# Cosine attention and a highway layer on one core: scores in 64x64 tiles, and a new order

## The chip, the core and the metric

The kernel runs on one core of one Trainium2 chip. The metric is the device time of one execution in microseconds. Engines are named as in the profile: PE (matrix products), PEld (its weight loads), DVE (VectorE), ACT (ScalarE), POOL (GpSimd), SP (SyncE, here only a queue of DMAs). A change of over 2% either way counts as faster or slower.

## The reference

```
q_n = q / (norm(q) + 1e-6);  k_n = k / (norm(k) + 1e-6)        # 8 batches, 12 heads, 448 tokens, 64 per head
attn = softmax(q_n @ k_n.T / tau)                              # tau 0.1
x = (attn @ v) as 3584 tokens x 768
out = T * relu(x @ w_h) + (1 - T) * x,   T = sigmoid(x @ w_t + b_t)
```

## The kernel before

Operands of the products are in fp16, sums in fp32. The work of a batch `b` is cut into 3 groups of 4 heads; a group holds two pairs `s` of heads, and the two heads `t` of a pair lie side by side in the partitions of the turned q and k (64 each). Tokens are split as `token = 7*l + j`, so 448 tokens are 7 blocks `j` of 64.

For each group: load q and k, square them (`sq`, ACT), sum (`rd`, DVE), inverse roots (`ln`/`ie` on ACT for batch 0, Newton steps `nt` on DVE later), scale to `qn` and `kn` (POOL mostly; `scale`), turn so that the 64 numbers of a head lie along the partitions (`turn`: on PE with a copy by DVE, or by a transposing DMA on SP for q from batch 3 and k from batch 5). Then for each pair: scores, transposed, as 128 keys x 448 queries (`qk`), exponentials by ACT (`exp`, tile `E`), products with v (`av` for three blocks of 128 queries, `avt` for the last 64), a division (`rc`, `ev` on DVE) into `x`. Column 64 of `vp` is one, so the same product gives the sum of the exponentials. Per head 448 keys are three blocks of 128 and one of 64. The 64 left over of both heads of a pair are put together: `kn` has an eighth block, half of it zero, so that one product with 128 rows (`qkt`, line 507, tile `Et`) gives the left-over scores of both heads.

PE runs in modes, named in the code: F is the whole array, T two tiles of 64 rows x 128 columns (the two heads of a pair at once), C two tiles of 128 rows x 64 columns.

Batch 0 is done in smaller pieces (`attend0`), one step for 128 queries, to get going early. `wm` and `wf` are products of zeros (tile `wz`) that fill PE's early gaps. Each batch's `x` (4 tiles of 128 tokens x 768, the last a half) goes through `ffn`: a transpose to `xT` (DMA on SP from batch 1), 24 products `ff` for T and H, then `za`, `hm`, `gt`, `gg` on DVE, `th` on ACT, `out` on POOL and a store on SP. The layer's work of a batch is spread over the attention of later ones.

Nothing is scheduled by rule: `ORDER` is a table of numbers that lists all operations in the order in which they are issued, `SLOTS` the buffer of each tile. Each engine runs its own part of this list in order. Two rules add waits without data: an SP load of q waits for the last ACT operation ahead of it in the list, and the first POOL operation of certain kinds behind a DVE operation of such kinds (`PORT`) waits for that one.

Of the kernel before, what the change touches and what calls it, by code (L numbers as in the profile page):

```python
# [126 lines left out]
    ),  # L127
}


# [733 lines left out]
```

## Time and profile before

| | |
|---|---|
| median of 3 runs | 255.94 us (255.06 to 262.05) |
| span of the profiled execution, first to last instruction | 252.9 us |
| PE, ACT, DVE, POOL busy, share of the span | 94%, 84%, 82%, 73% |
| PE matmuls | 2895 |
| PE's granted clock, mean | 0.990 |

The profile shows the span and not the profiled execution's whole time; the median of the runs is 3.0 us above that span, the lowest run 2.2 us. In the profile a matmul's duration includes the time until its result has drained, so durations of neighbours overlap and their sum says nothing: the cost of one is the distance from its start to the next one's start, called its pitch below.

### The profile page before, as it was taken

What the parts mean: (1) busy time and instruction counts of PE and PEld (TensorE: products, weight loads), DVE (VectorE), ACT (ScalarE), POOL (GpSimd) and SP (SyncE); (2) the same over time, 40 slices, a digit from 0 to 9 for tenths busy, and PEclk for the clock granted to TensorE, in tenths of its full rate; (3) what the DMA queues carried; (4) which work ended last, traced back from release to release, by engine and by line L of the source; (5) the groups of instructions that cost most, each with busy time, mean ns of one, the idle gap of its engine ahead of it and who ended that gap; (6) DMA issues with size and microseconds to landing.
All of it is one profiled execution on the core that took longest, in us unless ns stands there. A gap on an engine that the chain in (4) does not pass through costs nothing.

```text
span 252.9 us, 7457 instructions
## 1 busy us (share of the span) xinstructions
PE 237.5 (94%) x2895; PEld 147.1 (58%) x2895; DVE 208.0 (82%) x462; ACT 211.5 (84%) x421; POOL 184.0 (73%) x261
## 2 busy tenths in 40 slices
PE   5959999999999999989999999999999999999990
PEld 2425776557756665645765566656656655675650
DVE  4977989999999999989899869689767665556983
ACT  3589999999999999989999999999997669981120
POOL 8369599959798979796989775878476983522540
PEclk9997999999999999999999999999999999999998
DMA  6999999999589999999999998999779588745755
GB/s 219 286 270 237 288 259 202 200 271 179 72 104 146 314 264 248 151 223 163 266 157 170 156 114 138 249 207 193 128 129 231 93 135 192 162 127 123 187 147 156
DMA packets 75892, 47.78 MB, mean 189 GB/s; under 512 B 51536, under 2 KB 72656, under 8 KB 75856
## 3 DMA queue, kind: packets, MB, share of 16 engines
q1 hardware_dynamic: 55568, 33.86, 59.2%
q0 software_dynamic: 19856, 12.68, 37.1%
q10 hardware_dynamic: 432, 0.75, 0.8%
q8 instruction: 22, 0.36, 0.6%
q14 instruction: 14, 0.11, 0.1%
HBM read 38.34 MB, written 11.01 MB: 195 GB/s over the span
## 4 chain that ended last, share of the span: by engine, by line
PE 68%; DMA 11%; ACT 8%; DVE 7%; issue 2%; POOL 2%; SPq 0%; DVEq 0%; POOLq 0%; ACTq 0%
PE B L682 26%; PE B L496 10%; PE B L526 8%; DMA xT<-x 7%; PE B L679 5%; PE B L521 3%; DMA E<-in_k_dram 3%; PE B L447 3%; ACT E L502 3%; PE B L534 3%; PE B L507 2%; PE B L573 2%; ACT sq L380 2%; PE B L305 2%; DVE hm L720 1%
## 5 line engine op out<-in xcount | busy, mean ns | idle before, releaser
L502 ACT ACTIVATE E<-B 128x448 f16<-128x448 f32 x252 | 122.8, 612 | 9.6 <-PE B L496 8.6
L682 PEld LDWEIGHTS <-xT 128*128 128x128 f16 x576 | 52.1, 98 | 39.6 <-issue 6.9
L752 POOL TENSOR_TENSOR os<-x,hm 128x384 f32<-128x384 f16 x53 | 47.6, 912 | 29.8 <-DVE hm L747 21.3
L682 PE MATMUL B<-wh,xT 128*128 128x384 f16 x288 | 56.7, 326 | 0.6 <-DMA xT<-x 0.6
L682 PE MATMUL B<-wt,xT 128*128 128x384 f16 x288 | 55.0, 326 | 1.8 <-DMA xT<-x 1.4
L432 POOL TENSOR_TENSOR kn<-kr,y 128x192 f16<-128x192 f16 (+1 forms) x84 | 45.8, 562 | 10.6 <-DVE y L409 6.1
L391 DVE TENSOR_REDUCE n<-sq 128x14 f32<-128x896 f32 (+1 forms) x50 | 51.2, 1039 | 2.8 <-ACT sq L380 2.6
L432 POOL TENSOR_TENSOR qn<-qr,y 128x448 f16<-128x448 f32 x47 | 43.9, 946 | 9.1 <-ACT y L420 4.4
L526 PE MATMUL B<-vp,E 128*128 128x65 f16 x756 | 38.7, 193 | 0.0
L724 ACT ACTIVATE tt<-z 128x768 f16<-128x768 f32 (+1 forms) x32 | 26.3, 821 | 14.6 <-DVE z L711 14.5
L720 DVE SCALAR_TENSOR_TENSOR hm<-B,x 128x384 f16<-128x384 f32 x53 | 28.8, 549 | 8.4 <-PE B L682 3.9
L526 PEld LDWEIGHTS <-E 128*128 128x128 f16 x756 | 33.7, 98 | 3.2
L496 PE MATMUL B<-qT,kT 64*128 64x448 f16 x252 | 34.8, 354 | 0.4 <-DVE hm L720 0.4
L711 DVE TENSOR_TENSOR z<-B,bias 128x384 f32<-128x384 f32 x48 | 25.8, 551 | 9.3 <-PE B L682 6.3
L521 PE MATMUL B<-vp,Et 128*128 128x130 f16 x126 | 28.1, 223 | 0.0
L380 ACT ACTIVATE sq<-qr 128x896 f32<-128x896 f32 (+1 forms) x24 | 24.1, 1022 | 3.5 <-DMA qr<-in_q_dram 3.5
L509 ACT ACTIVATE Et<-B 128x448 f16<-128x448 f32 x42 | 26.1, 631 | 0.4 <-PE B L507 0.4
L542 DVE SCALAR_TENSOR_TENSOR x<-B,rd 128x448 f16<-128x448 f32 x42 | 25.6, 618 | 0.9
L337 POOL DMA_DIRECT2D vr<-in_v_dram x32 | 21.9, 690 | 2.5 <-DVE z L711 2.5
L586 ACT ACTIVATE E<-B 128x512 f16<-128x512 f32 (+1 forms) x42 | 20.6, 607 | 0.9 <-POOL qn L432 0.5
L380 ACT ACTIVATE sq<-kr 128x896 f32<-128x896 f16 x17 | 17.0, 1041 | 1.1 <-DMA kr<-in_k_dram 1.1
L305 PE MATMUL B<-wz 128*128 128x512 f16 x39 | 14.7, 433 | 2.6 <-DVE wz L281 2.6
(81 smaller groups left out, 313.7 us busy)
## 6 DMA issues: line engine op xcount, KB each, us to landing
out_dram<-os SPq DMA_DIRECT2D x47, 192.0 KB, 3.3
qr<-in_q_dram SPq DMA_DIRECT2D x6, 1344.0 KB, 8.3
kr<-in_k_dram POOLq DMA_DIRECT2D x7, 672.0 KB, 11.6
vr<-in_v_dram POOLq DMA_DIRECT2D x16, 192.0 KB, 6.9
qr<-in_q_dram SPq DMA_DIRECT2D x6, 448.0 KB, 10.0
vr<-in_v_dram POOLq DMA_DIRECT2D x16, 144.0 KB, 7.7
out_dram<-os SPq DMA_DIRECT2D x15, 96.0 KB, 3.8
wt<-in_moe_w_t_dram POOLq DMA_DIRECT2D x1, 1152.0 KB, 24.4
```

Source lines behind the costliest of these rows:

```text
L380: nc.scalar.activation(dst, src, AF.Square, scale=sc)
L391: nc.vector.reduce_sum(R("n2", b)[:, c : c + 7 * n], a, axis=AX.X)
L432: ENG[eng].tensor_mul(N[:, :, t, :] if nm == "q" else N[:, lo > 0 : (lo > 0) + 2 * (hi - lo) - 1 : 2, t, :], source(nm, b, g)[:, t, 64 * l ...
L496: nc.tensor.matmul(R("B", ("S", n, c, t))[:, 0:S], lhsT=R("kT", i)[ln, s, 128 * c : 128 * c + 128], rhs=queries(ln), start=True, stop=True)
L502: nc.scalar.activation(R("E", n)[:, at : at + 7, :].rearrange("l j x -> l (j x)"), R("B", ("S", n, c, t))[:, 0:S], AF.Exp)
L509: op("ACT", f"expt {n}", lambda: nc.scalar.activation(R("Et", n).rearrange("l j x -> l (j x)"), R("B", ("St", n))[:, 0:S], AF.Exp), r=[("B ...
L521: nc.tensor.matmul(U[:, 2 * c : 2 * c + 2, :], lhsT=Et[:, 2 * c : 2 * c + 2, :].rearrange("l j x -> l (j x)"), rhs=vp[:, 6:8, 0:65], start ...
L526: nc.tensor.matmul(U[:, 2 * c + t, :], lhsT=E[:, at : at + 2, :].rearrange("l j x -> l (j x)"), rhs=vp[:, 3 * t + m, 0:65], start=False, s ...
L682: nc.tensor.matmul(P[:, 0:MH], lhsT=xT[:, cc, :], rhs=w_[:, cc, MH * mh : MH * mh + MH], start=(cc == 0), stop=(cc == CC - 1))
L720: op("DVE", f"hm {g} {mh}", lambda at=at, sl=sl, mh=mh: nc.vector.scalar_tensor_tensor(out=R("hm", g)[:, sl], in0=R("B", at)[:, 0:MH], sca ...
L724: op("ACT", f"th{nb} {g}", lambda: nc.scalar.activation(R("tt", g)[:, 0:W], R("z", g)[:, 0:W], AF.Tanh, scale=0.5), r=[("z", g), ("t0",)], ...
L752: op(eng, f"out {g} {mh}", lambda sl=sl, mh=mh: ENG[eng].tensor_add(R("os", g)[:, sl], xpart(mh), R("hm", g)[:, sl]), r=[("gg", g), xk], w ...
```

## The change

The scores are now computed as four tiles of 64 keys x 64 rows at once (mode Q, `score`), two heads by two halves of the keys. The blocks of keys stay in the order of the tokens, `kn` has seven blocks and no zeros. The block that is left over is block 3 for pair 0 and block 6 for pair 1, so one step of four tiles (`tails`) gives the left-over scores of all four heads of a group: for each head `t` a bank of PSUM with pair 0 in the lower and pair 1 in the upper half, and `Et` is kept by group and head. `av` takes its left-over product per head (65 columns) instead of one for both (130). The zeros that this needs are in `vp`. `kn` is scaled in one instruction instead of two, k turned in 7 blocks instead of 8, and by one DMA instead of two.

```diff
-    WARM, NF, NLATE = 18, 39, 2
+    WARM, NF, NLATE = 18, 60, 2
-    SCALE = {("q", 0, 0): ("DVE", "POOL"), ("k", 0, 0): ("DVE", "POOL")}
+    SCALE = {(nm, 0, g): ("DVE", "POOL") for nm in "qk" for g in range(NG)}
...
-        Et=(3, [128, 7, 64], FP16), ...
+        Et=(4, [128, 7, 64], FP16), ...
...
-            for lo, hi in ((0, 7),) if nm == "q" else ((0, 4 - t), (4 - t, 7)):
...
+            def fn(t=t, eng=eng):
+                c = col(nm, g) + 7 * t
+                ENG[eng].tensor_mul(R(nm + "n", i)[:, :, t, :], source(nm, b, g)[:, t].rearrange("l (j d) -> l j d", d=D),
+                                    R("y", b)[:, c : c + NJ].unsqueeze(2).to_broadcast([128, NJ, D]))
...
+    def score(out, o, w, K, Q, s, c):
+        for t, h in ((0, 0), (1, 1), (0, 1), (1, 0)):
+            ln = slice(64 * t, 64 * t + 64)
+            S_, j = (s, c + h * (4 - s)) if c < NC else (h, 3 + 3 * h)
+            nc.tensor.matmul(out[t][64 * h : 64 * h + 64, o[t] : o[t] + w], lhsT=K[ln, j, S_, :], rhs=Q[ln, :, S_, :], start=True, stop=True)
...
-                for t in range(2):
-                    ln = slice(64 * t, 64 * t + 64)
-                    nc.tensor.matmul(R("B", ("S", n, c, t))[:, 0:S], lhsT=R("kT", i)[ln, s, 128 * c : 128 * c + 128],
-                                     rhs=queries(ln), start=True, stop=True)
+                score([R("B", ("S", n, c, t)) for t in range(2)], (0, 0), S, R("kT", i), R("qT", i), s, c)
...
-            nc.tensor.matmul(R("B", ("St", n))[:, 0:S], lhsT=R("kT", i)[:, s, 384:512], rhs=queries(slice(0, 128)), start=True, stop=True)
+            score([R("B", ("St", i, t)) for t in range(2)], (0, 0), S, R("kT", i), R("qT", i), 0, NC)
...
-            nc.tensor.matmul(U[:, 2 * c : 2 * c + 2, :], lhsT=Et[:, 2 * c : 2 * c + 2, :].rearrange("l j x -> l (j x)"),
-                             rhs=vp[:, 6:8, 0:65], start=True, stop=False)
             for t in range(2):
-                for m in range(NC):
...
+                for m in range(NC + 1):
+                    lt = E[:, 7 * (2 * m + t) + 2 * c :][:, 0:2] if m < NC else R("Et", (i, t))[:, 2 * c : 2 * c + 2]
...
-                    ld_kf(g, "SP" if g else "ACT")
+                    ld_kf(g, "ACT")
...
-            ld_qk("q", b)
+            for g in range(NG):
+                ld_qk("q", b, [g])
...
-                elif o.held:
-
-                    behind(made[0], act)
-                elif o.port and o.eng == "DVE":
-                    before = made[-1]
-                elif o.port and before is not None:
-
-                    behind(made[0], before)
-                    before = None
+                last[o.seq] = made[-1]
+                if o.seq in BEHIND:
+                    behind(made[0], last[BEHIND[o.seq]])
```

`BEHIND` is a table of 61 waits written out: 47 of a POOL operation for a DVE operation a few places ahead of it (the rule of before made 48), and 14 of an SP load of q for an ACT operation. v is loaded by pair instead of by head, with the same sizes. `ORDER` and `SLOTS` are new throughout:

```diff
-66 1 67 342 68 0 69 3 72 71 7 70 5 42 61 339 23 19 75 74 64 21 44 52 20 51 22 55 79 9 83 43 2 6 14 13 81 82 73 80 8 85
+0 84 92 4 2 9 86 13 345 16 88 5 85 17 12 3 91 14 87 6 18 1 89 7 22 8 10 93 20 21 15 90 11 97 99 19 23 349 24 98 25 26
```

Three places of the order follow. First PE, at a step of scores in the middle of the program; `kT` and `qT` are the turned operands, B the banks of PSUM. Before, two products for the two heads of a pair, then the left-over product of another pair:

```order
L496 LDWEIGHTS kT_90
L496 MATMUL B_124<-qT_89,kT_90 128x448
L496 LDWEIGHTS kT_90
L496 MATMUL B_128<-qT_89,kT_90 128x448
L507 LDWEIGHTS kT_91
L507 MATMUL B_123<-qT_87,kT_91 128x448
```

Now, one step (the four tiles of 64 keys alternate between the two heads' banks):

```order
L459 LDWEIGHTS kT_93
L459 MATMUL B_125<-qT_89,kT_93 64x448
L459 LDWEIGHTS kT_93
L459 MATMUL B_124<-qT_89,kT_93 64x448
L459 LDWEIGHTS kT_93
L459 MATMUL B_125<-qT_89,kT_93 64x448
L459 LDWEIGHTS kT_93
L459 MATMUL B_124<-qT_89,kT_93 64x448
```

There are 126 such steps for `qk` as before, and 21 instead of 42 steps for the left-over blocks, each now of this form.

Second POOL, at the scaling of batch 0 (`qn`, `kn` from the loads `qr` and `E`, which holds batch 0's k; `vr`, `vp` are v as loaded and as used). Before:

```order
L432 TENSOR_TENSOR qn_83<-qr_61,y_78 128x7x64
L432 TENSOR_TENSOR kn_66<-E_94,y_78 128x4x64
L432 TENSOR_TENSOR kn_66<-E_94,y_78 128x3x64
L432 TENSOR_TENSOR qn_84<-qr_61,y_78 128x7x64
L432 TENSOR_TENSOR kn_67<-E_95,y_78 128x4x64
L432 TENSOR_TENSOR qn_84<-qr_61,y_78 128x7x64
L432 TENSOR_TENSOR kn_67<-E_95,y_78 128x3x64
L478 COPY vp_71<-vr_69 64x6x64
L432 TENSOR_TENSOR kn_67<-E_95,y_78 128x3x64
L432 TENSOR_TENSOR kn_67<-E_95,y_78 128x4x64
```

Now:

```order
L433 TENSOR_TENSOR qn_83<-qr_61,y_78 128x7x64
L433 TENSOR_TENSOR kn_66<-E_94,y_78 128x7x64
L325 DMA kr_64<-in_k_dram 128x6x448
L433 TENSOR_TENSOR qn_84<-qr_61,y_78 128x7x64
L433 TENSOR_TENSOR kn_67<-E_95,y_78 128x7x64
L433 TENSOR_TENSOR kn_68<-E_96,y_78 128x7x64
L433 TENSOR_TENSOR qn_85<-qr_61,y_78 128x7x64
L474 COPY vp_71<-vr_69 64x2x3x64
```

The other half of groups 1 and 2 (`qn_84`, `kn_67`, `qn_85`, `kn_68`) went to DVE, and the copy of v stands behind all of the scaling.

Third SP, around the transposes of batch 2's `x`. Before:

```order
L322 DMA qr_61<-in_q_dram 128x6x448
L759 DMA out_dram<-os_120 64x384 x2
L762 DMA out_dram<-os_117 64x768 x2
L662 DMA_TRANSPOSE xT_106<-x_103 128x6x128
L662 DMA_TRANSPOSE xT_109<-x_103 128x6x128
L662 DMA_TRANSPOSE xT_105<-x_103 128x6x128
L762 DMA out_dram<-os_119 64x768 x2
L662 DMA_TRANSPOSE xT_107<-x_103 128x3x128
```

Now:

```order
L327 DMA qr_61<-in_q_dram 128x2x448
L442 DMA_TRANSPOSE qT_86<-qn_85 128x7x128
L746 DMA out_dram<-os_120 64x768 x2
L327 DMA qr_61<-in_q_dram 128x2x448 x2
L646 DMA_TRANSPOSE xT_107<-x_104 128x6x128
L646 DMA_TRANSPOSE xT_110<-x_104 128x6x128
L646 DMA_TRANSPOSE xT_109<-x_104 128x6x128
L746 DMA out_dram<-os_118 64x768 x2
```

The load of q is in three parts, with a transpose and stores between them. At the start of the program, PE now has 44 products of zeros ahead of its first transpose, before 34, and the other 11 of the 21 added ones stand among the work of batch 0; the tile of zeros is the first that DVE writes, before it came behind one `vp`. The three loads of batch 0's k are issued by ACT behind its table load; before, one was issued by ACT ahead of it and two by SP.

More of the change, by code (lines that the diff above doesn't have):

```diff
@@ new lines @@
+    "qT": "01232013210310230123013",
+    "kT": "01232013201320123012301",
+    "E": "012012102101021002210210202102120102120210212021021021102",
+    "Et": "012301230101230123012301230123012301230123",
+    "rd": "010101010101011010101001010101010101010101010101010101",
+    "x": "012012012",
+    "xT": "01234012340214302130421304321430",
+    "z": "01011010100010101011010110010101",
+    "tt": "01010101001100101011010001001011",
+    "hm": "01202021012110121022102120010210",
+    "os": "01231200132032302033020201320321",
@@ L131 @@
+BEHIND = dict(
+    map(int, n.split(":"))
+    for n in """
[5 rows of a table added]
+""".split()
+)
 PORT = ("nt", "gt", "gg", "vc", "qn", "kn", "vt", "out", "cx", "ou")
@@ L440, in turn @@
         at = ("T" + nm, i)
-        nj = NJ if nm == "q" else 8
-        def fn():
-            T = R16(at)[:, 0 : 128 * nj].rearrange("p (s j l) -> p j s l", s=2, j=nj)
-            for j in range(nj):
-                nc.tensor.transpose(T[:, j], R(nm + "n", i)[:, j].rearrange("l t d -> l (t d)"), ident[:, :])
-        if nm == "q" and b in QDMA:
-            op("SP", f"xd7 {b} {g}", lambda: nc.sync.dma_start(
-                R("qT", i).rearrange("p s x -> p (s x)").rearrange("p (j x) -> p j x", j=NJ),
-                R("qn", i).rearrange("l j t d -> l (j t d)"), transpose=True), r=[("qn", i, 0), ("qn", i, 1)], w=[tn(nm, i)])
-            return
@@ L453, in turn @@
-        if nm == "k" and b in KDMA:
-            for s in range(2):
-                op("SP", f"xdk {b} {g} {s}", lambda s=s: nc.sync.dma_start(
-                    R("kT", i)[:, s, :].rearrange("p (j x) -> p j x", j=8),
-                    R("kn", i)[64 * s : 64 * s + 64].rearrange("l j t d -> l (j t d)"), transpose=True),
-                   r=[("kn", i, 0), ("kn", i, 1), ("zkn",)], w=[tn(nm, i)])
-            return
-        op("PE", f"t{nm} {b} {g}", fn, r=[(nm + "n", i, 0), (nm + "n", i, 1), ("id",)] + ([("zkn",)] if nm == "k" else [])
+        if b in (QDMA if nm == "q" else KDMA):
+            op("SP", f"xd7{nm} {b} {g}", lambda: nc.sync.dma_start(
+                R(nm + "T", i).rearrange("p j s l -> p j (s l)"),
+                R(nm + "n", i).rearrange("l j t d -> l (j t d)"), transpose=True), r=[(nm + "n", i, 0), (nm + "n", i, 1)], w=[tn(nm, i)])
+            return
@@ L461, in turn @@
+        def fn():
+            for j in range(NJ):
+                nc.tensor.transpose(R16(at)[:, 128 * j : 128 * j + 128], R(nm + "n", i)[:, j].rearrange("l t d -> l (t d)"), ident[:, :])
+        op("PE", f"t{nm} {b} {g}", fn, r=[(nm + "n", i, 0), (nm + "n", i, 1), ("id",)]
            + ([("wm",)] if i == 0 and nm == "k" else []), w=[("B", at)], mode="F")
         op("DVE", f"cp{nm} {b} {g}", lambda: nc.vector.tensor_copy(
-            turned(nm, i), R16(at)[:, 0 : 128 * nj].rearrange("p (s x) -> p s x", s=2)), r=[("B", at)], w=[tn(nm, i)])
+            turned(nm, i).rearrange("p j s l -> p (j s l)"), R16(at)[:, 0:896]), r=[("B", at)], w=[tn(nm, i)])
@@ L550, in attend0, with at @@
     def attend0(g, i):
-        q_, k_ = turned_of(g)
-        w = 128 if i < 3 else 64
+        K_, Q_ = lambda: turned("k", g), lambda: turned("q", g)
+        nj = 2 if i < 3 else 1
+        w = 64 * nj
         e = ("q0", g, i)
-        def unit(s):
-            o = 896 * s if i < 3 else 0
-            h = 0 if i < 3 else 192 * s
-            return [[o + 512 * t + h + w * c for c in range(NC)] for t in range(2)], o + 384 + (0 if i < 3 else 64 * s)
+        def at(s, t, m):
+            if i < 3:
+                return (0, 768)[s] + (384, 512)[s] * t + w * m if m < NC else 768 + 512 * t + 384
+            return 448 * t + (192 * s + w * m if m < NC else 384)
@@ L561, in flat, with queries, fq @@
         def flat():
             return R("E", e).rearrange("l j x -> l (j x)")
+        def queries():
+            return Q_()[:, 2 * i : 2 * i + nj]
         for ss in ((0,), (1,)) if i < 3 else ((0, 1),):
-            A, B_ = (("S0", g, i, ss[0], t) for t in range(2))
-            o = unit(ss[0])[0][0][0]
-            def fq(ss=ss, A=A, B_=B_, o=o):
+            A = [("S0", g, i, ss[0], t) for t in range(2)]
+            base = [at(ss[0], t, 0) for t in range(2)]
+            M = 384 if ss == (0,) else 512 if ss == (1,) else 448
+            def fq(ss=ss, A=A, base=base):
@@ L581, in attend0 @@
-            n = f"{g} {i} {ss[0]}"
-            op("PE", f"qk0{len(ss)} {n}", fq, r=[tn("q", g), tn("k", g)],
-               w=[("B", A), ("B", B_)], mode="T")
-            op("PE", f"qt0{len(ss)} {n}", ft, r=[tn("q", g), tn("k", g)], w=[("B", A, "t")], mode="F")
-            for t, X, m in ((0, A, 512), (1, B_, 384)):
-                op("ACT", f"ex{m} {n}", lambda X=X, m=m, t=t, o=o: nc.scalar.activation(
-                    flat()[:, o + 512 * t : o + 512 * t + m], R("B", X)[:, 0:m], AF.Exp),
-                   r=[("B", X)] + ([("B", X, "t")] if t == 0 else []), w=[("E", e, s) for s in ss])
+                        score([R("B", a) for a in A], [at(s, t, c) - base[t] for t in range(2)], w, K_(), queries(), s, c)
@@ new lines, in ft @@
+            def ft(A=A, base=base):
+                score([R("B", a) for a in A], [at(0, t, NC) - base[t] for t in range(2)], w, K_(), queries(), 0, NC)
+            n = f"{g} {i} {ss[0]}"
+            op("PE", f"qk0{len(ss)} {n}", fq, r=[tn("q", g), tn("k", g)], w=[("B", a) for a in A], mode="Q")
+            if ss != (0,):
+                op("PE", f"qt0{len(ss)} {n}", ft, r=[tn("q", g), tn("k", g)], w=[("B", a, "t") for a in A], mode="Q")
+            for t in range(2):
+                op("ACT", f"ex{M} {n} {t}", lambda X=A[t], M=M, o=base[t]: nc.scalar.activation(
+                    flat()[:, o : o + M], R("B", X)[:, 0:M], AF.Exp),
+                   r=[("B", A[t])] + ([("B", A[t], "t")] if ss != (0,) else []), w=[("E", e, s) for s in ss])
@@ L595, in full @@
                 def full(s=s):
-                    vp, U, (at, tl) = R("vp", 0)[:, 2 * g + s], U_(), unit(s)
-                    nc.tensor.matmul(U[:, :, s], lhsT=flat()[:, tl : tl + 128], rhs=vp[:, 6:8, 0:65], start=True, stop=False)
+                    vp, U = R("vp", 0)[:, 2 * g + s], U_()
                     for t in range(2):
-                        for m in range(NC):
-                            nc.tensor.matmul(U[:, t, s], lhsT=flat()[:, at[t][m] : at[t][m] + 128],
-                                             rhs=vp[:, 3 * t + m, 0:65], start=False, stop=(t == 1 and m == NC - 1))
-                op("PE", f"av0 {g} {i} {s}", full, r=[("E", e, s), ("vp", 0, 2 * g + s), ("vp", 0, 6)], w=[("B", u)], mode="F")
+                        for m in range(NC + 1):
+                            a = at(s, t, m)
+                            nc.tensor.matmul(U[:, t, s], lhsT=flat()[:, a : a + w], rhs=vp[:, 3 * t + m if m < NC else 6 + t, 0:65],
+                                             start=(m == 0), stop=(m == NC))
+                op("PE", f"av0 {g} {i} {s}", full, r=[("E", e, 0), ("E", e, 1), ("vp", 0, 2 * g + s), ("vp", 0, 6, s)], w=[("B", u)], mode="F")
             op("DVE", f"rc {g} {i} 0", lambda: nc.vector.reciprocal(
@@ L632, in attend0 @@
                r=[("B", u), ("rd", e)], w=[("x", 0, i)])
-    def turned_of(g):
-        return lambda: turned("q", g), lambda: turned("k", g)
     def ffn(b, i):
@@ L801 @@
             for p in range(NP):
+                if p % 2 == 0:
+                    tails(b, p // 2)
                 scores(b, p)
@@ L812 @@
         with tc.manual_schedule():
-            before = act = None
+            last = {}
             for o in pl.ordered(ORDER, SLOTS):
```

122 lines of the change are left out of this document (46 added, 76 removed), and 149 rows, old and new, of tables (BEHIND, ORDER).

## The prediction

> **What bounds the kernel now.** I read the head of the page first.
>
> ```profile
> span 252.9 us, 7457 instructions
> PE 237.5 (94%) x2895; PEld 147.1 (58%) x2895; DVE 208.0 (82%) x462; ACT 211.5 (84%) x421; POOL 184.0 (73%) x261
> ```
>
> Then busy time in stretches of 10 us (columns: PE, PEld, DVE, ACT, POOL busy with the number of instructions, granted clock, DMA share, GB/s).
>
> ```profile
> 20.00:30.00 10.00, 10.00 (x140) 6.38 (x138) 9.24 (x23) 9.12 (x19) 6.90 (x11) 0.86 1.14 265
> 60.00:70.00 10.00, 10.00 (x175) 7.17 (x173) 9.46 (x20) 10.00 (x23) 8.57 (x14) 1.00 0.72 94
> 100.00:110.00 10.00, 8.55 (x107) 5.11 (x104) 9.72 (x25) 9.49 (x19) 8.54 (x13) 1.00 1.09 161
> 190.00:200.00 10.00, 9.56 (x118) 5.97 (x117) 6.98 (x13) 8.26 (x19) 7.32 (x10) 1.00 1.13 198
> 230.00:240.00 10.00, 10.00 (x64) 6.04 (x62) 8.34 (x18) 1.78 (x3) 5.14 (x6) 1.00 0.79 183
> ```
>
> Behind the start PE is hardly ever idle, and at 230 it works alone on the layer that is left: it sets the end. But ACT is as full through the middle, so PE cannot simply go ahead. Pitches decide, so I took a piece of PE's timeline (start, length, then the group).
>
> ```profile
> 186.06 0.22 PE L521 MATMUL B<-vp,Et 128*128 128x130 f16 x1
> 186.12 0.35 PE L526 MATMUL B<-vp,E 128*128 128x65 f16 x6
> 186.31 0.35 PE L507 MATMUL B<-qT,kT 128*128 128x448 f16 x1
> 186.59 0.28 PE L534 MATMUL B<-vp,E 128*64 128x65 f16 x6
> 186.71 0.20 PE L534 MATMUL B<-vp,Et 128*64 128x65 f16 x2
> 186.84 0.74 PE L496 MATMUL B<-qT,kT 64*128 64x448 f16 x6
> 187.51 3.10 PE L682 MATMUL B<-wt,xT 128*128 128x384 f16 x18
> 190.45 0.35 PE L507 MATMUL B<-qT,kT 128*128 128x448 f16 x1
> 190.64 0.22 PE L521 MATMUL B<-vp,Et 128*128 128x130 f16 x1
> ```
>
> From starts alone: a left-over product takes 0.19 us (190.45 to 190.64) and 0.28 where the next one is in another mode (186.31 to 186.59), so a change of mode costs 0.09. Three pairs of score products take 0.67, less 0.09 is 0.19 a pair: two tiles cost what one product does. The 18 layer products have 0.163 each. An `av` block is 0.25: 0.06 for the 130 columns and 0.19 for six of 65, 0.032 each. The eight products of `avt` take 0.25 less 0.09, 0.02 each.
>
> **The change on PE.** Left-over steps: 42 x 0.19 = 8.0 us go and 21 x 0.19 = 4.0 come, if four tiles of 64x64 run at once as two of 64x128 do: -4.0. The 126 `qk` steps stay at 0.19 on the same condition. An `av` block becomes eight products of 65 columns, 0.256 for 0.25: 126 + 18 blocks x 0.006 = +0.9. Batch 0's scores are 84 short steps for 96, at much the same few hundredths each: 0, give or take 1. Changes of mode, counted along both written orders, are 184 before and 182 now: -0.2.
>
> ```profile
> 36.08 0.45 PE B L447 x8
> ```
>
> In the chain of work eight transposes take 0.45 us, so the fifteen eighth blocks of k that go are worth 15 x 0.056 = -0.8. Together PE's work falls by 4.1 us, beside the products of zeros.
>
> The four tiles at once are what no row shows, and bounds are far apart: nothing extra, or a second round of 0.19 for each of 147 steps, 28 us. Two tiles beside each other in rows (`qk`) and two in columns (`avt`, two outputs at once) both run at full rate, so I take nothing extra.
>
> [...]
>
> **How much of it reaches the end.** ACT's pitches:
>
> ```profile
> 101.69 1.98 ACT L502 ACTIVATE E<-B 128x448 f16<-128x448 f32 x4
> 103.38 1.11 ACT L380 ACTIVATE sq<-qr 128x896 f32<-128x896 f32 x1
> 104.22 1.14 ACT L502 ACTIVATE E<-B 128x448 f16<-128x448 f32 x2
> ...
> 108.03 1.02 ACT L724 ACTIVATE tt<-z 128x768 f16<-128x768 f32 x1
> 108.77 0.72 ACT L509 ACTIVATE Et<-B 128x448 f16<-128x448 f32 x1
> ```
>
> An exponential is 0.42 us, a square 0.84, a tanh 0.74. Their numbers are the same before and after (252 + 42 exponentials of 448 columns, batch 0's again with the same columns in all). So there is a second bound: ACT's work up to some exponential, and from there PE's work from the first product that needs it. Priced with these pitches along both orders, the largest such sum is 230.2 us before (in the middle, at pair 17) and 228.8 now. By this bound only 1.4 of the 4.1 us come through; the rest sits where PE waits for ACT. I take 1.4, with 4.1 as the other end, since ACT's full rows say that this chain is tight.
>
> **Stalls in the middle.** PE loses time at three places:
>
> ```profile
> 106.64 0.35 PE L507 MATMUL B<-qT,kT 128*128 128x448 f16 x1
> 108.43 0.34 PE L682 MATMUL B<-wt,xT 128*128 128x384 f16 x1 [1.45 <-DMA xT<-x]
> 140.54 0.35 PE L526 MATMUL B<-vp,E 128*128 128x65 f16 x6
> 141.45 0.66 PE L682 MATMUL B<-wh,xT 128*128 128x384 f16 x3 [0.56 <-DMA xT<-x]
> 197.18 0.35 PE L496 MATMUL B<-qT,kT 64*128 64x448 f16 x1 [0.44 <-DVE hm L720]
> ```
>
> And the transposes of `x` about the first place (issue time on SP, then the time to landing):
>
> ```profile
> L662 SPq DMA_TRANSPOSE xT<-x x4: 1211/1238/1256, 98.1 to 102.1; - x4
> DMA to landing us min/median/max: 2.8/5.5/8.7
> ```
>
> Two of them end on a transposed `x` that came late: 1.6 us and 0.7 us of starts; the third is 0.4. At the first, transposes issued from 98.1 on took up to 8.7 us to land. The new order leaves them more room: PE work between the issue of a transpose of `x` and its first use, priced as above, is at least 3.4 us and 7.5 in the median, before 0.9 and 6.0; for turned q and k the least is 5.6, before 4.3. That q comes in thirds lets SP put transposes between them; what else is gained there by fewer DMAs (9 of k for 18, 1.24 us of SP each) meets 12 more issues of loads. I take 2.5 us of 2.7 gone; the other end is a loss of 2, since a new order can put a late landing somewhere else, and 8.7 us is longer than most of that room.
>
> **The start.**
>
> ```profile
> 9.59 1.05 DVE L432 TENSOR_TENSOR qn<-qr,y 128x448 f16<-128x448 f32 x1
> 17.30 0.57 ACT L586 ACTIVATE E<-B 128x512 f16<-128x512 f32 x1
> 17.73 0.50 POOL L478 COPY vp<-vr 64x384 f16<-64x384 f16 x1 [1.95 <-DMA vr<-in_v_dram]
> 18.19 1.53 POOL L432 TENSOR_TENSOR kn<-E,y 128x192 f16<-128x192 f32 x3
> 19.32 1.03 PE L447 MATMUL B<-ident,kn 128*128 128x128 f16 x8 [2.54 <-POOL kn L432]
> L285 ACT ACT_TABLE_LOAD x2 | 2.6, 1283 | 1.3 <-PEq L845 1.3
> ```
>
> Before, POOL stood 1.95 us at the copy of v with half of a k behind it, and PE waited 2.54 us for that (then came the low clock of 20 to 30). Now the copy is behind the scaling and DVE has half of it, so this wait goes. Next late is DVE: four more products of 1.05 us, 4.2, among its sums and copies, which is more than the 2.54 that PE waited; so I do not count the second group's k as earlier. Ten more products of zeros ahead of the first transpose, at
>
> ```profile
> 9.29 0.81 PE L305 MATMUL B<-wz 128*128 128x512 f16 x3
> 9.94 0.38 PE L301 MATMUL B<-wz 128*128 128x512 f16 x1
> ```
>
> 0.22 us each, hold it back by 2.2 us at most (PE starts sooner, its tile of zeros being the first that DVE writes); ACT's first exponential, at 17.30 behind squares that it had to do anyway, hides that, and if this cover is gone it costs what is left of the 2.2. The three loads of k behind ACT's table load may come later by its length, 1.28 us. The other eleven zeros, 2.4 us, lie in gaps in which PE waits for ACT. I take -0.5 us, between -2.5 and +1.5.
>
> **POOL** is off the path:
>
> ```profile
> L432 POOL TENSOR_TENSOR kn<-kr,y 128x256 f16<-128x256 f16 x42 | 25.4, 612 | 3.8 <-DVE hm L747 2.3 <-DVE y L409 1.2 <-DVE tt L726 0.3
> L432 POOL TENSOR_TENSOR kn<-kr,y 128x192 f16<-128x192 f16 x42 | 21.3, 512 | 6.7 <-DVE y L409 4.8 <-DVE tt L726 1.2 <-DVE hm L747 0.5
> ```
>
> 64 columns more cost 100 ns, so one of 448 is 0.91 us where two were 1.12: 42 times, 9 us less work. It has 27% idle time, so I count nothing. The written waits of POOL for DVE (47 for 48) change little.
>
> **Sum.** -1.4 (chain) - 2.5 (stalls) - 0.5 (start) = -4.4 us: the span goes from 252.9 to 248.5, and with the 3.0 us between span and median, 255.9 to **251.5 us**.
>
> **Rivals.**
> - *PE alone sets the pace*: all 4.1 us come through and the start gives its 2.5 us: -4.1 - 2.5 - 2.5 = -9.1, some of it overlapping: about 247.5 us. For it: at 190 to 200 ACT is idle and takes up slack. Against: ACT's full rows before that.
> - *The order does not hold on the chip*: new late landings cost 2 us instead of saving 2.5, start +1: 255.9 - 1.4 + 2 + 1 = 257.5, down to 254 where only one happens. For it: landings of 8.7 us.
> [...]
> - *Slower: the four tiles run in two rounds*, because two column tiles of one row half cannot stream at once. Price 0.19 us for each of 147 steps: 251.5 + 28 = 279 us. It decides from 65 ns more per step on: (4.4 + 5.1) / 147. For it: no row has all four. Against: either half alone runs at full rate.
>
> **How the numbers follow.** Forecast 0.52 (249 to 254), PE alone 0.17 (246 to 250), order 0.16 (254 to 258), loads 0.09 (253.5 to 257), two rounds 0.06. From 247 to 257.5 leaves out 0.06 above with two rounds, and about 0.12 at both edges. Two per cent, about what a measurement of this kernel can tell from no change, is 5.1 us: faster means under 250.8, which PE alone and two fifths of the forecast give, 0.17 + 0.21 = 0.38; slower means over 261, two rounds and a little of a bad order, 0.08; the same 0.54.
>
> **What would show it.** Right: a step of four tiles with a pitch of 0.19 us and its starts within some 20 ns, no PE wait of over 1 us for `xT`, no wait of PE for POOL at the start, ACT as full as before from 30 to 190, POOL busy some 10 us less. Wrong: steps of 0.21 or 0.38 us; a first exponential of batch 0 later than 17.3; ACT with idle time in the middle, which would mean that PE or a DMA sets the pace and my 1.4 is too small or the stalls moved.

## The result

The changed kernel takes **251.6 us** (251.11 to 252.33 in five runs); before, 255.94. The ratio is 0.989, with a 95% interval of 0.985 to 0.993, and two more comparisons with other runs gave 0.987 [0.983, 0.991] and 0.990 [0.984, 0.995]. So it is 1.1% faster, within the 2% that count as no change here, and its median is 0.1 us from the forecast. Medians count every execution and ratios leave out the slow ones, among them one of 573.8 us of the changed kernel, whose profile is not read here; by the ratio the gain is 2.8 us (1.7 to 3.8). The span went from 252.9 to 249.6 us, 3.3 us less. The other microsecond between the two medians is not the kernel's work: in every execution whose span is on record, of either kernel, the time is 1.7 to 1.9 us above that span. So the profiled execution of before took about 254.7 us (an estimate from its span), 1.2 us less than the median of 255.94.

The head of the page after:

```profile
span 249.6 us, 8704 instructions
PE 238.2 (95%) x3507; PEld 149.2 (60%) x3507; DVE 207.2 (83%) x459; ACT 211.0 (85%) x421; POOL 173.1 (69%) x210
```

POOL is busy 10.9 us less, where 9 were priced. PE has 612 products more and is as full as before. The same five stretches of 10 us (PE, PEld, DVE, ACT, POOL, granted clock, DMA share, GB/s):

```profile
20.00:30.00 10.00, 8.99 (x206) 5.59 (x204) 9.21 (x25) 10.00 (x19) 5.36 (x8) 1.00 1.14 273
60.00:70.00 10.00, 10.00 (x185) 6.89 (x184) 9.86 (x19) 10.00 (x23) 8.84 (x11) 1.00 0.96 159
100.00:110.00 10.00, 9.94 (x145) 6.53 (x145) 9.79 (x23) 10.00 (x22) 8.00 (x11) 1.00 1.24 136
190.00:200.00 10.00, 10.00 (x173) 6.37 (x173) 5.94 (x13) 9.27 (x21) 8.52 (x11) 1.00 1.22 193
230.00:240.00 10.00, 10.00 (x63) 6.02 (x62) 9.03 (x21) 3.37 (x4) 4.33 (x5) 1.00 0.59 147
```

The low clock of 20 to 30 (0.86) is gone, and PE and ACT are now both full at 100. Where the time came out can be followed from the starts of the exponentials of full blocks (252 in all, read from the records):

```
exponential no.      1     36     72    108    144    180    216    252   end of PE
before            42.7   67.7   94.8  122.0  148.0  175.3  199.3  225.7   246.5
after             41.0   69.7   95.5  121.9  148.3  173.0  197.4  222.2   243.4
```

By these starts alone nothing is gained up to the 144th, at 148 us. But the new order also puts ACT's other work in other places, so what ACT has still ahead of it has to be counted in. At the start of the 36th exponential that is 152.9 us before and 151.2 now, at the 108th 99.8 and 99.0, at the 144th 74.7 and 72.5. With it, the changed kernel is 0.3 us behind at the 36th, 0.9 ahead at the 108th, 1.9 ahead at the 144th and 3.1 at the end of PE. Between the 36th and the 144th ACT stood idle for 2.1 us before and does not now. The largest of these waits came right behind the late transpose of `x` that held PE at 108.43 us:

```profile
110.65 0.54 ACT L502 ACTIVATE E<-B 128x448 f16<-128x448 f32 x1 [1.16 <-PE B L496]
```

Three steps of four tiles in PE's timeline after (start, length, group):

```profile
190.87 0.76 PE L459 MATMUL B<-qT,kT 64*64 64x448 f16 x12
191.56 0.28 PE L525 MATMUL B<-vp,E 128*64 128x65 f16 x6
```

Twelve products in 0.69 us, where six took 0.67 before (186.84 to 187.51). Four tiles of 64x64 run at once. Over the steps that another step follows, the pitch has two values: 213 ns for the first step behind a change of mode (53 steps), 189 for the ones behind it (27, and two longer ones). Before it was 200 and 189. The first and the last start of a step lie 10 ns apart in the median. A product's record is longer than its pitch (a left-over product of before 353 ns in the mean, at 190 from start to start); what the rest of the record covers, no run shows.

One kind of gap is new. At three places PE stops in the middle of an operation, and no releaser is named but its own issue:

```profile
28.84 0.39 PE L589 MATMUL B<-vp,E 128*128 128x65 f16 x7
30.05 0.20 PE L589 MATMUL B<-vp,E 128*128 128x65 f16 x1 [0.82 <-issue]
...
35.16 0.46 PE L459 MATMUL B<-x 64*64 64x128 f16 x24
36.24 0.32 PE L459 MATMUL B<-x 64*64 64x64 f16 x16 [0.63 <-issue]
...
57.61 0.41 PE L612 MATMUL B<-vp,E 128*64 128x65 f16 x14
58.87 0.22 PE L612 MATMUL B<-vp,E 128*64 128x65 f16 x2 [0.85 <-issue]
```

One late transpose of `x` holds PE now, at another place, and for less:

```profile
206.28 0.99 PE L666 MATMUL B<-wt,xT 128*128 128x384 f16 x5 [0.56 <-DMA xT<-x]
```

At the start ACT's first exponential came 1.8 us earlier (15.51 for 17.30), and DVE's scaling of 448 columns took 0.62 us where it took 1.05:

```profile
10.10 0.62 DVE L433 TENSOR_TENSOR qn<-qr,y 128x448 f16<-128x448 f32 x1
...
15.51 1.85 ACT L575 ACTIVATE E<-B 128x512 f16<-128x512 f32 x4 [1.35 <-PE B L459]
```

### The profile page after: what moved, and what is told of

It is laid out like the page before. It is cut to its first block, busy times and chain, and to the rows that moved or that the text cites. A ratio compares the mean times of both kernels' runs of the same rounds, so it can differ in the third digit from the quotient of the medians.

```text
span 249.6 us, 8704 instructions
## 1 busy us (share of the span) xinstructions
PE 238.2 (95%) x3507; PEld 149.2 (60%) x3507; DVE 207.2 (83%) x459; ACT 211.0 (85%) x421; POOL 173.1 (69%) x210
## 4 chain that ended last, share of the span: by engine, by line
PE 64%; DMA 9%; ACT 9%; DVE 8%; POOL 4%; issue 3%; SPq 1%; DVEq 0%; ACTq 0%
PE B L666 31%; PE B L459 12%; PE B L517 11%; DMA qr<-in_q_dram 7%; ACT E L489 4%; PE B L663 3%; PE B L449 3%; PE B L525 3%; POOL qn L433 2%; ACT E L575 2%; DMA xT<-x 2%; DVE z L695 2%; ACT sq L383 2%; POOL kn L433 1%; PE B L589 1%
## 5 line engine op out<-in xcount | busy, mean ns | idle before, releaser
L489 ACT ACTIVATE E<-B 128x448 f16<-128x448 f32 x252 | 124.9, 666 | 5.6 <-PE B L459 5.4
L433 POOL TENSOR_TENSOR qn<-qr,y 128x448 f16<-128x448 f32 x45 | 41.5, 935 | 17.3 <-DVE y L412 7.0
L459 PE MATMUL B<-qT,kT 64*64 64x448 f16 (+2 forms) x812 | 47.1, 320 | 0.1
L433 POOL TENSOR_TENSOR kn<-kr,y 128x448 f16<-128x448 f16 x42 | 39.1, 938 | 5.6 <-DVE tu L408 2.0
L517 PEld LDWEIGHTS <-E 128*128 128x128 f16 x756 | 35.0, 97 | 7.6 <-issue 3.4
L517 PE MATMUL B<-vp,Et 128*128 128x65 f16 x252 | 35.0, 191 | 0.0
L459 PEld LDWEIGHTS <-kT 64*64 64x64 f16 x812 | 19.3, 105 | 19.0 <-issue 12.2
L383 ACT ACTIVATE sq<-qr 128x896 f32<-128x896 f32 (+1 forms) x24 | 25.8, 1073 | 5.6 <-DMA qr<-in_q_dram 5.4
L517 PEld LDWEIGHTS <-Et 128*128 128x128 f16 x252 | 24.8, 99 | 0.0
L575 ACT ACTIVATE E<-B 128x512 f16<-128x512 f32 (+2 forms) x42 | 20.3, 580 | 2.1 <-PE B L459 1.9
```

The source lines that it names most:

```text
L383: nc.scalar.activation(dst, src, AF.Square, scale=sc)
L433: ENG[eng].tensor_mul(R(nm + "n", i)[:, :, t, :], source(nm, b, g)[:, t].rearrange("l (j d) -> l j d", d=D), R("y", b)[:, c : c + NJ].unsq ...
L459: nc.tensor.matmul(out[t][64 * h : 64 * h + 64, o[t] : o[t] + w], lhsT=K[ln, j, S_, :], rhs=Q[ln, :, S_, :], start=True, stop=True)
L489: nc.scalar.activation(R("E", n)[:, at : at + 7, :].rearrange("l j x -> l (j x)"), R("B", ("S", n, c, t))[:, 0:S], AF.Exp)
L517: nc.tensor.matmul(U[:, 2 * c + t, :], lhsT=lt.rearrange("l j x -> l (j x)"), rhs=vp[:, 3 * t + m if m < NC else 6 + t, 0:65], start=(m == ...
```

## The experiments

Each starts from the changed kernel. Ratios are to the kernel before on the same chip; without an edit the ratio is 0.9886 (mean of the three), and 0.001 is a quarter of a microsecond. Two entries below are that kernel again:

> The changed kernel once more, without an edit, beside the next three: 0.989 of the time before, and the three stalls of 0.8 us inside a unit at the same products of PE (28.8, 35.4 and 57.6 us); the span says how far one profile differs from another.

> The changed kernel without an edit on the same chip as the two kernels with one store, 0.988 of the time before; its profile says how far spans, waits and stalls differ from one execution to the next: the stalls at products 478 and 862 of PE are there again, the wait for a transposed x at 205 us is 0.5 to 2 us.

Measured: 250.86 us, 0.987, and 251.88 us, 0.990. The second one's span is 249.4, with the gaps of PE that end at 35.8 and 58.2 us at the same products, the latter 0.59 for 0.85. The one at 30 us is not there. The profile of the first is the one that is not read.

### Pairs again

```diff
     def score(out, o, w, K, Q, s, c):
+        if w == S and c < NC:
+            for t in range(2):
+                ln = slice(64 * t, 64 * t + 64)
+                nc.tensor.matmul(out[t][:, o[t] : o[t] + w], lhsT=K[ln, c].rearrange("p s l -> p (s l)"), rhs=Q[ln, :, s, :],
+                                 start=True, stop=True)
+            return
```

> The 126 full-width score steps run as two products of 64x128 (one per row half, 128 adjacent stationary columns: the keys of both sequences of one block, so the scores are of other keys) where the changed kernel has four of 64x64; the left-over steps and batch 0 keep four tiles. In the trace of the changed kernel a step of four has a pitch of 188 or 213 ns (median 213), in that of before a step of two 188 or 200 ns (median 200). Theory A (a step of four tiles pays about 13 ns more than one of two, by its number of products): back-to-back steps come back to a median of 200 ns, which is 126 x 0.013 = 1.6 us less, while 22 more changes of mode (204 for 182) add 22 x 0.093 = 2.0 us: 251.6 within 1 us, or ratio 0.985 to 0.994. Theory B (the longer pitch belongs to the place in the new order, such as banks that come free late): the median stays at 213 ns and the kernel is 2 us slower, 253.6, ratio 0.997. Beside that 252 products and their 252 weight loads go; if PE's stalls of 0.8 us inside a unit (at 28.8, 35.4 and 57.6 us) come at fixed numbers of its instructions, the first two, which lie ahead of nearly all of these steps, stay where they are, and the third moves to a later product.

Measured: 251.88 us, 0.988 [0.983, 0.994], span 249.0. The first step of a run is back at 200 ns, the later ones stay at 189: theory A, with 13 ns that are paid once in a run of steps and not per step. In time the two forms do not differ within the interval, about 1.5 us either way; as pairs also bring 22 more changes of mode, this run does not price the tiles by themselves, and the pitches do. So what the 64x64 form brings is the left-over step that serves four heads.

### The left-over step twice

```diff
         def ft():
             score([R("B", ("St", i, t)) for t in range(2)], (0, 0), S, R("kT", i), R("qT", i), 0, NC)
+            score([R("B", ("St", i, t)) for t in range(2)], (0, 0), S, R("kT", i), R("qT", i), 0, NC)
```

> The left-over step of each of the 21 groups is issued twice in a row into the same banks, so the 21 steps that the change took away are back as PE work: 21 x 0.19 to 0.21 = 4.0 to 4.5 us. Theory A (PE sets the end from about 40 us on, since it hardly ever idles there): all of it comes out at the end, 251.6 + 4.0 to 4.5 = 255.6 to 256.1, ratio about 1.005. Theory B (the chain on which the forecast rested: ACT up to about pair 17, then PE): only the 15 steps behind pair 17 count, 2.9 to 3.2 us: 254.6, ratio 1.000 to 1.002. Theory C (the saving of left-over steps is not what made the kernel faster): 251.6 to 252.5. The two steps in a row, the first of which nobody waits for, also give the pitch of a step of four by itself: 189 ns if a step costs what one product of 448 columns does, 213 if loads or tiles queue.

Measured: 254.06 us, 0.995 [0.991, 0.999], so 1.6 us more than the unedited kernel by the ratios (give or take 1) and 2.5 by the span (252.1). That is 40 to 60% of the 4.0 us of PE work: less than A's 4.0 to 4.5, a little under B's 2.9 to 3.2, and more than C's 0 to 0.9, though the lower end of the interval, 0.6 us, reaches into C. The doubled steps add 19 pitches of 189 ns and 3 of 213: a step costs what one product of 448 columns does.

### PE work left out, early and late

```diff
+                            if not tail and b in (0, 1) and w_ is wh and cc % 5:
+                                continue
                             nc.tensor.matmul(P[:, 0:MH], lhsT=xT[:, cc, :], rhs=w_[:, cc, MH * mh : MH * mh + MH],
```

The late cut has `(5, 6)` for `(0, 1)`.

> In batches 0 and 1 the products of the second weight are cut from six to two for each half of the columns (left out: four of six terms of that sum): 2 batches x 3 groups x 2 halves x 4 products x 0.163 = 7.8 us of PE work less, at 38 to 105 us. Theory A (PE alone sets the end from 40 us on): all of it comes out, 251.6 - 7.8 = 243.8, ratio 0.958. Theory B (the chain of the forecast: ACT's work up to about pair 17 of 42, then PE's): ACT is full from 40 to 160 us already, so nearly nothing comes out, 250.6 to 251.6, and PE then shows idle time that ends on ACT. In between would mean that the two bounds are only a few us apart.

> The same cut in batches 5 and 6: 7.8 us of PE work less, at about 170 to 225 us. Theory A (PE alone): -7.8, 243.8, ratio 0.958. Theory B (ACT up to about pair 17 to 34, then PE): -6 to -7.8, since ACT's chain up to a late exponential lies 7 us below the largest: 243.8 to 245.6. The pair with the early cut is what tells: the same work, worth 7.8 us in one place and nothing in the other by B, and the same in both by A.

Measured: early 250.69 us, 0.987 [0.983, 0.991]; of 7.8 us of PE work 0.4 comes out by the ratio, 1.4 at most by the interval. The profiled span, 247.3 us, is 2.3 shorter, but it is that of the shortest of its executions. Theory A is out. Late 252.83 us, 0.996 [0.993, 0.999]: slower by 2 us, which neither theory expected. PE's and SP's timelines with the late cut, and a stretch of windows:

```profile
202.50 1.78 PE L459 MATMUL B<-qT,kT 64*64 64x448 f16 x12
207.50 2.74 PE L668 MATMUL B<-wt,xT 128*128 128x384 f16 x8 [3.22 <-DMA xT<-x]
```

```profile
199.41 1.36 SPq L442 DMA_TRANSPOSE qT<-qn  x1
200.86 1.39 SPq L748 DMA_DIRECT2D out_dram<-os  x2
202.34 2.70 SPq L646 DMA_TRANSPOSE xT<-x  x2
```

```profile
207.00:212.00 5.00, 4.50 (x22) 2.27 (x26) 1.05 (x3) 0.19 (x1) 0.79 (x1) 0.68 0.85 196
```

`x` of batch 6 is complete at 200.1 us (end of its last scaling on DVE), its transposes are issued from 202.34 on and land some 5 us later, the first at 207.46. In the changed kernel `x` is complete at 201.5, and yet the same two transposes are issued earlier and the first lands at 206.23:

```profile
201.91 3.36 SPq L646 DMA_TRANSPOSE xT<-x  x2
```

With the cut, SP still had a transpose of q and two stores to issue when `x` was ready. Products that were cut stand ahead of this point in PE's order, so PE arrives earlier and the transfer comes 1.2 us later: PE waits, and then runs five microseconds at a granted clock of 0.68. So the late cut does not show what PE work is worth there: it took the cover off a transfer.

### ACT work left out

```diff
+                    k = 5 if b in (2, 3) else 7
-                    nc.scalar.activation(R("E", n)[:, at : at + 7, :].rearrange("l j x -> l (j x)"), R("B", ("S", n, c, t))[:, 0:S],
+                    nc.scalar.activation(R("E", n)[:, at : at + k, :].rearrange("l j x -> l (j x)"), R("B", ("S", n, c, t))[:, 0 : 64 * k],
                                          AF.Exp)
```

> In batches 2 and 3 an exponential of a full block takes five of the seven blocks of queries (left out: the scores of the last two, whose old weights stay): 72 exponentials of 320 columns for 448. By batch 0's exponentials (0.371 us for 384 columns, 0.477 for 512, so 0.83 ns a column) each is 0.106 us shorter, 7.6 us of ACT in all, between 70 and 122 us, as much as the early cut took from PE. That cut brought nothing. Theory A (ACT alone sets the pace there, so PE's work is free): ACT's cut comes out nearly whole, 251.5 - 7 = 244 to 246. Theory B (PE and ACT are level: PE has only 0.4 us of idle starts per 10 us in that stretch, ACT 0.3, so neither cut alone can come out): 250.5 to 251.9, PE without stalls and ACT with some 7 us of idle time from 70 to 122. In between: ACT ahead by that much.

Measured: 251.93 us, 0.984 [0.977, 0.990]: 1.3 of 7.6 us, and 3.0 at most by the interval. The profile's span is 252.2 us. The stretch from 70 to 122 us, of the changed kernel, of the early PE cut and of this one:

```profile
70.00:122.00 52.00, 51.74 (x758) 32.71 (x757) 50.35 (x107) 52.00 (x106) 46.56 (x55) 1.00 1.20 197
```

```profile
70.00:122.00 52.00, 50.60 (x723) 31.07 (x723) 49.95 (x107) 52.00 (x107) 45.62 (x54) 1.00 1.13 207
```

```profile
70.00:122.00 52.00, 51.62 (x786) 32.09 (x783) 49.81 (x105) 46.94 (x106) 44.91 (x52) 1.00 1.04 188
```

With less PE work ACT is as full as before; with less ACT work ACT falls to 46.94 and PE is as full as before. So neither is ahead of the other: theory B. A third engine is not excluded: DVE is busy 50.35, 49.95 and 49.81 us in the same stretches, and no run takes work from it. The chain of work of this last run goes over PE, then over DVE, and then over the landing of one transposed `x`:

```profile
103.01 8.05 DMA xT<-x
```

That several engines are level here, whichever they are, is why neither cut gives much.

### Ten zeros fewer

```diff
-        op("PE", f"wf {i}", lambda i=i: nc.tensor.matmul(...),
+        op("PE", f"wf {i}", lambda i=i: 14 <= i < 24 or nc.tensor.matmul(...),
```

> The last ten products of zeros ahead of PE's first transpose are left out (34 for 44, as many as before). They take 10 x 0.22 = 2.2 us. In the changed kernel the first transpose starts at 13.10 us, the first exponential at 15.51, and ACT stands 1.35 us for PE there. Theory A (the zeros delay the start and the start sets all that follows): the first transpose comes up to 2.2 us earlier, the first exponential up to 1.35 us, and the time falls by as much: 250.2 to 250.8. Theory B (what sets the pace up to 60 us is ACT's and PE's work of the first batches, and the first exponential's place does not matter): 251.6 within 0.6. Theory C (the zeros keep the clock up): the granted clock falls under 0.95 in some stretch of 10 to 40 us and the time does not fall. On the stalls of 0.8 us inside a unit at 28.8, 35.4 and 57.6 us: if they sit at fixed numbers of PE's instructions (705, 961 and 1729 by count, 256 apart or multiples of it, as when code comes in blocks of 256), they move to the product that is 10 products (20 instructions) further on in the program; if they belong to a buffer or a place in the order, they stay at the same product.

Measured: 253.55 us, 0.994 [0.990, 0.999], span 251.0. PE's timeline:

```profile
12.05 0.56 PE L449 MATMUL B<-ident,qn 128*128 128x128 f16 x7 [1.75 <-POOL qn L433]
...
28.80 0.31 PE L459 MATMUL B<-qT,kT 64*64 64x128 f16 x8
29.75 0.25 PE L459 MATMUL B<-qT,kT 64*64 64x128 f16 x4 [0.64 <-issue]
...
57.61 0.19 PE L525 MATMUL B<-vp,Et 128*64 128x65 f16 x2
59.64 0.57 PE L459 MATMUL B<-qT,kT 64*64 64x448 f16 x8 [1.83 <-issue]
...
207.73 0.99 PE L666 MATMUL B<-wt,xT 128*128 128x384 f16 x5 [1.68 <-DVE vp L464]
```

The first transpose came 1.05 us earlier (12.05 for 13.10; it then waits for POOL) and the first exponential 0.75 us. None of it reached the end, so theory A is out; the clock stayed at 1.00, so C is out as well. B has the start right, but not the time, which is 1.5 us longer by the ratios. The gaps moved. In the changed kernel the first and last are inside `av0` and the batch 0 `avt`; here each is ten products further on in the program. Counted from the first product of PE, all three come behind number 350, 478 and 862, in both kernels. These numbers are 128 and 3 x 128 apart, and each product comes with one weight load (3507 of each), so the gaps lie whole multiples of 256 instructions apart. I take them for ends of blocks of 256 instructions: **PE waits for its own code**. Whatever operation stands there, the gap behind 478 is in all seven other edited kernels with two stores, the one behind 862 in six of them (not with q whole), the one behind 350 in five (not with pairs, nor with the early cut). The transfers of the instruction queue (count, MB, share; before, then after):

```profile
q8 instruction: 22, 0.36, 0.6%
```

```profile
q8 instruction: 27, 0.44, 0.7%
```

That is 16 KB each.

The packet records bear it out. Counted in steps of 128 products, 256 instructions, from number 94 on, the changed kernel has 27 boundaries and the one before 22, as many as there are transfers. Transfers end at 28.57, 34.83 and 57.14 us, and 1.4 to 1.7 us behind each of these ends PE goes on (30.05, 36.24 and 58.87). Why the kernel before has no such gap fits as well: the 128 products ahead of the three gaps took PE 5.3, 5.6 and 4.8 us, while before, with the same places counted, none of these stretches took less than 7.8. One other stretch in the changed kernel is as short, 5.4 us from 66.8 on, and has no gap; its transfer started 0.4 us behind its boundary, those ahead of the gaps 3.0 to 3.8.

The three gaps differ from run to run: here 0.64, 1.46 and 1.83 us, in the changed kernel 0.82, 0.63 and 0.85; with the wait at 207.7 that is 2.7 us more, which covers the 0.75 us gained at the start and the 1.4 us of span lost. That compares one execution of each kernel; why the gaps were longer in this one stays open.

### q in one load again

```diff
-            else:
+            elif b < 2:
                 ENG[eng].dma_start(d[:, gs[0] :: 3, :], a[:, :, gs[0] :: 3, :])
+            elif gs[0] == {2: 2, 3: 2, 4: 1, 5: 1, 6: 2, 7: 2}[b]:
+                ENG[eng].dma_start(d[:, :, :], a)
```

> From batch 2 on q comes in one load, at the place of its first third; the two other thirds are left out as instructions of SP. Theory A (the thirds let SP put transposes of x, q and k between them, which is why the late transposes of before are gone): waits of PE for xT of over 0.7 us come back at one or more places and the time rises by 1 to 2.5 us, 252.6 to 254.1. Theory B (the new order alone did that, the pieces do not matter): 251.6 within 0.6, no wait for xT of over 0.7 us besides the one of 0.8 at 205. Theory C (fewer DMAs help): 250.6 to 251.2.

Measured: 255.25 us, 1.006 [1.003, 1.009]: 4.4 us more than the unedited kernel by the ratios, 2.4 by the span. SP at batch 7's load of q, with whole q and then in the changed kernel, and the wait that follows on PE with whole q:

```profile
150.53 0.54 SPq L329 DMA_DIRECT2D qr<-in_q_dram  x1
152.15 5.25 SPq L649 DMA_TRANSPOSE xT<-x  x3
```

```profile
150.21 0.60 SPq L327 DMA_DIRECT2D qr<-in_q_dram  x1
151.94 3.90 SPq L646 DMA_TRANSPOSE xT<-x  x3
```

```profile
158.57 1.15 PE L669 MATMUL B<-wt,xT 128*128 128x384 f16 x6 [1.97 <-DMA xT<-x]
```

Behind three times the bytes, SP spends 5.25 us on three transposes instead of 3.90, part of it in waits for their operands. From issue to landing they take 6.4, 5.5 and 6.1 us, in the changed kernel 3.6, 3.2 and 4.8, and PE waits 1.97 us. Over the whole kernel its waits for `xT` are three, 3.9 us in all, where the changed kernel has one of 0.56. Theory A, and more than it expected.

### GpSimd no longer waits for VectorE

```diff
-                if o.seq in BEHIND:
+                if o.seq in BEHIND and o.eng == "SP":
```

> The written waits of POOL for DVE (and all others but those of SP) are left out; order and work stay. In the trace of the changed kernel a DVE scaling of 448 columns takes 0.62 us at 9.5 to 10.1 us while POOL waits; before, one took 1.05 beside POOL's own scaling. Theory A (the two slow each other and it matters): DVE's scalings at 9 to 20 us go back to about 1.05 us, the first exponential comes 0.4 to 1 us later than 15.5, and the time rises by 0.5 to 1.5 us, 252.1 to 253.1. Theory B (they slow each other, but DVE and POOL have idle time and the end does not see it): DVE products of 1.05 us beside POOL's, and 251.6 within 0.5. Theory C (the waits cost more than they bring, as POOL stands 3 to 4 us at each): 250.6 to 251.3.

Measured: **277.54 us**, 1.087 [1.080, 1.094]. All three theories are out by an order of size. DVE, POOL and PE at 81 us:

```profile
81.55 6.60 DVE L731 TENSOR_TENSOR hm<-tt,hm 128x768 f16<-128x768 f16 x1
```

```profile
81.92 0.95 POOL L433 TENSOR_TENSOR qn<-qr,y 128x448 f16<-128x448 f32 x1
82.82 0.94 POOL L433 TENSOR_TENSOR kn<-kr,y 128x448 f16<-128x448 f16 x1
83.71 1.82 POOL L433 TENSOR_TENSOR qn<-qr,y 128x448 f16<-128x448 f32 x2
85.50 0.90 POOL L736 TENSOR_TENSOR os<-x,hm 128x384 f32<-128x384 f16 x1
86.37 0.92 POOL L433 TENSOR_TENSOR qn<-qr,y 128x448 f16<-128x448 f32 x1
```

```profile
88.68 1.04 PE L459 MATMUL B<-qT,kT 64*64 64x448 f16 x4 [5.26 <-DVE z L695]
```

One gate product of DVE, 0.60 us in the mean of the changed kernel, takes 6.60: it ends only behind POOL's row of six operations, and PE stands 5.26 us behind it. DVE is busy 24.6 us more in all, most of it in this product and three other operations of 3.10, 5.23 and 5.97 us. Between the six, which follow each other without a pause, VectorE's product did not end; why, the trace does not show. At the start, where I looked for the effect, the first exponential comes no later (14.96 us). The kernel before had such waits too, 48 of them, so having them is not what the change brought.

### One store for two

From 190.5 to 205.3 us SP's issues stand in a row in the changed kernel, so I halved the number of stores, by themselves and beside the late cut. (The row is not issue time alone: SP's own waits for POOL, DVE and PE from 190 to 208 us come to 7.7 us.)

```diff
-                for h in range(2):
-                    nc.sync.dma_start(rows[2 * i + h], O[64 * h : 64 * h + 64, :])
+                nc.sync.dma_start(rows[2 * i : 2 * i + 2], O[:, :])
```

> SP stores the rows of a group in one DMA where it issued two (0.6 us of SP each): 28 issues of about 0.6 us less. In the changed kernel SP issues without a gap from 190.5 to 205.3 us (transposes of 1.2 to 1.7 us and stores of 1.24 a pair), and PE waits 0.8 us at 205.3 for the transposed x that is the last of this row. Theory A (SP's row of issues sets when that x is turned): four stores stand in it, so the transposes come 2 to 2.5 us earlier against ACT's exponentials, the wait at 205.3 goes, and 0.8 to 1.5 us come out: 250.1 to 250.8 where the changed kernel has 251.6. Theory B (SP only waits there for what POOL and DVE give it, or one store of twice the size takes twice the issue): within 0.5 us of the changed kernel and the wait stays.

> One store per group and, beside it, the cut of batches 5 and 6 (four of six terms of the second weight's products left out), which by itself, with two stores, brought nothing: PE waited 3.8 us for a transposed x at 203.5 us and ran its products at half pace behind it. Theory A (SP's row of issues was what ate the cut): the wait falls to under 1.5 us and at least 3 of the 7.8 us come out: 248.5 or less. Theory B (ACT or the landing of the transposes ate it): the wait stays at 3 us or more and the time is 251 to 253.

Measured: 382.45 us, 1.505 [1.500, 1.510], and with the late cut 380.6, 1.497 [1.489, 1.505]. SP saved issues, and the kernel lost 131 us. From the waits and SP's timeline of the first:

```profile
POOL os L736 <- DMA out_dram<-os: 53.2, 10, 9.6
PE B L666 <- DMA xT<-x: 53.0, 7, 16.1
```

```profile
106.71 13.01 SPq L646 DMA_TRANSPOSE xT<-x  x3
```

In the packet records, the 128 rows of 3 KB of one store take 7.5 to 12 us with about two of them under way at once; stored in two halves of 64 rows, 1.5 to 4.6 us with 4 to 15 at once. The destination's outer dimension is now 2; why about two packets are under way at a time, the runs do not show. SP spends 13.01 us on three transposes at 106.71, and PE waits 53.0 us in all for a transposed `x`, where the unedited kernel has one wait of 0.56. A fourth gap inside an operation, of 5.56 us, stands behind product 1374 there, 4 x 128 behind 862; that this is code held up behind the stores is likely, but not shown. Whether SP's row costs time at 200 us was thereby not answered, and stays open.

## Why the prediction was right, and where it was not

The median came within 0.1 us of the forecast, and that is partly luck. The gain was forecast as 4.4 us; by the ratio it is 2.8 (1.7 to 3.8) and by the span 3.3. The rest of the 4.3 us between the medians is mostly that the median of before lay 1.2 us above the execution that was profiled. Within the span, terms that were off compensated each other. The mechanism, four tiles at once and a smaller part of PE's saving at the end, held.

**PE's work.** Right. Steps of four tiles run at once, and with two tiles or four the time is the same within the interval (0.988 and 0.9886 of the time before). The rival of two rounds is out: doubled steps come at 189 ns. The chance for loads (0.09) and the steps of 0.21 us named as a sign of being wrong rest on a time for weight loads that no run shows. What the runs showed are steps of 213 ns in 53 of 80, so that sign did appear, but once per run of steps and not in each. There two tiles took 200 before: 53 runs x 13 ns = 0.7 us that I had not counted.

**How much reaches the end: 1.4 of 4.1.** That only a part comes through holds, and the size is perhaps a little low: put back, 4.0 us of left-over steps cost 1.6 us by the ratios (give or take 1) and 2.5 by the span. The rival that PE alone sets the pace fell with the early cut. My picture of why was too simple. It had ACT alone as the bound of the first part; the cut of ACT's work shows that PE is level with it, and perhaps DVE, so that neither PE nor ACT alone gives much there.

**Stalls: -2.5.** What went is right, what came was missing. The three waits of 2.7 us went as forecast, and ACT's idle time from its 36th to its 144th exponential, 2.1 us, went with them. But PE got two gaps of 0.85 and 0.56 us behind 57 us; if these reach the end whole, which no run shows, about -1.3 is left. The step that I did not have is that 612 more products are more code (27 transfers of 16 KB for 22), and that PE, as I read its gaps, waits for it (0.63 to 0.85 us at three places). I also priced the thirds of q as neutral (SP's issues against more room); they are what keeps the transposes on time, 2.4 us by the span, 4.4 by the ratios.

**The start: -0.5.** PE's wait for POOL went, the first exponential came 1.8 us earlier, the granted clock from 20 to 30 us is 1.00 for 0.86. Yet the 36th exponential is 2.0 us later. Most of that is ACT's own work, which the new order puts earlier: from its first exponential to the 36th it is busy 28.0 of 28.6 us, where it was busy 25.0 of 25.0. Counted by the work that ACT has still ahead, the kernel is 0.4 us ahead at the first exponential and 0.3 behind at the 36th; the gaps of 0.82, 0.63 and 0.85 us lie between. That part of the gain at the start is worth nothing, the ten zeros show: 0.75 us earlier there, and later at the end. So the start's share is within half a microsecond of zero. By the same count 2.2 us come out between the 36th and the 144th exponential, where the stalls were, and 1.2 behind. This follows one engine's work and is not an experiment.

**The span.** It fell by 3.3 and not 4.4 us. The forecast added 3.0 us between span and median as if they were fixed; 1.7 to 1.9 us are, and the rest was the distance of one execution from the median of others.

## What to carry to other kernels

When two engines are both full through a stretch, work taken from one of them alone may be worth next to nothing there, as here (0.4 of 7.8 us from PE, 1.3 of 7.6 from ACT, by the ratios); find the stretch where the others have idle time, and price only the work that lies in it. Compare a profile's span with the time of its own execution, not with a median. Splitting products into smaller tiles kept the rate here (189 ns for a step behind another, of two tiles or four) but brought 612 products more, and the gaps inside an operation, multiples of 256 instructions apart and 1.4 to 1.7 us behind the end of a transfer of the instruction queue, I read as waits for the engine's own code. And work that looks spare in a written order may be covering a transfer, as the late cut showed (PE waited 3.22 us): before taking it out, ask what lands during it.
